# Four heads share one scaling in windowed attention, with earlier maxima in a fused feed-forward

## The chip, the cores and the metric

The kernel runs on one core of one Trainium2 chip. The metric is the device time of one execution in microseconds (us). Three runs of the kernel before gave 613.23, 614.52 and 616.42 us, so its median is 614.52 us.

## The reference

Two computations follow one another. The first is windowed attention: 4 batches, 8 heads, 768 positions, head size 64. Each query sees 8 global keys and the 96 latest keys up to itself, with a linear distance bias per head. The second is a feed-forward network on the 3072 x 512 result, with a leaky rectifier.

```python
scores = (1 / sqrt(64)) * q @ k.T + bias       # masked to 8 global and 96 local keys
a = exp(scores - max(scores)); a = a / (sum(a) + 1e-9)
x = (a @ v) as 3072 tokens x 512               # heads side by side
h = x @ w_in                                   # 512 -> 2048
g = maximum(h, 0) + alpha * minimum(h, 0)      # alpha per column
out = g @ w_out                                # 2048 -> 512
```

## The kernel before

The 3072 tokens are worked in twelve units u = 0 to 11 of 256 tokens. In a unit, each head h = 0 to 7 is attended (`attend`), the eight results stand side by side as `xn`, `xn` is transposed to `xt`, the first layer gives 16 blocks of 128 columns f = 0 to 15 and the second layer adds these 16 blocks up in two PSUM banks `o`. Almost every large product is three fp16 matmuls: a number is split into a high fp16 part (the "first copy", L342, L343, L351, L487) and the rest (L361, L362), and high by high, high by low and low by high are summed. The first two units keep fp32 in their attention and are transposed on TensorE; from unit 2 the transposes are DMAs.

**Attention.** TensorE makes scores `sp` (L609, L616), VectorE adds the bias and finds the extremum (L632), ScalarE exponentiates with a running sum (L637) into `pr`. In units 0 and 1, TensorE transposes `pr` into a bank `tp` (L657) and ScalarE copies that to `pt` (L661). `av` (L690) is the product with the values. The sums are inverted by two small VectorE instructions (L644, L646), and `xn` is `av` times the inverse (L699). `GROUP` says how many heads share one inversion and one multiplication.

**First layer.** For units 0 to 3, `ff_in2` makes two neighbouring blocks f in the two halves of one bank `h`, 12 matmuls each (L873). ScalarE (L342; L343 if it goes to VectorE) puts alpha times each half into `g`. VectorE takes the maximum with the whole bank (L881), and with it the bank is free. Then ScalarE casts the high part `gg` (L883) and VectorE makes the rest (L361). Units 0 and 1 have two banks with the tag `h`. From unit 4 on, `ff_in4` (L806 and on) uses sums of weight blocks `sw` and fewer products. The second layer is L897; L903 copies the finished bank and L906 stores it.

**Weights.** Each block f comes from memory as 64-bit numbers in two parts of 512 columns. Each part is turned into fp16 pairs by a first scaling `wf`, the bit work L478 (`wb`), L481 (`wb`) and L484 (`wf`) on VectorE, a first copy on ScalarE (L487) and the rest on VectorE (L362, `whl`). So a block costs VectorE eight instructions, beside units 0 and 1 only.

**Order.** Nothing is in loop order at the end. Every operation goes to a planner (`Plan`) with a key, a cost and the engine it may run on. The planner plays the program through with these costs: an engine that comes free takes the ready operation with the smallest key whose buffers are free, and the order found is the order that is written out. `slot` gives the key of a first-layer block; for unit 1 it stands `DELTA` behind unit 0's at the start and closer at the end. `mul` and `copy` belong to ScalarE, but the planner gives one to VectorE when ScalarE is far behind by its count (`FLEX`). So a changed key moves work between engines too. PSUM has eight banks: two `sp`, one `av`, one `ax`, two `h`, two `o`.

The squares (`energy`, L434) serve a check of the number range and are on ScalarE: `x_energy` squares a unit's `xt`, `weigh` the weights.

Of the kernel before, what the change touches and what calls it, by code (L numbers as in the profile page):

```python
# [23 lines left out]
P = 128  # L24
# [6 lines left out]
NU = 12  # L31
# [255 lines left out]
def c_dma(nbytes):  # L287
    return nbytes / 360.0
# [6 lines left out]
DELTA = 7  # L295
# [4 lines left out]
GROUP = (2, 2, 2, 2)  # L300
# [11 lines left out]
QLEAD = 2  # L312
SLEAD = 36
# [9 lines left out]
def fast(tc, cn, a):  # L323
    nc = tc.nc
    ctx = ExitStack()
    with ctx:
# [112 lines left out]
        def weigh(f, key):  # L439

            w = whl[f]
            for part in range(2):
                energy(key, lambda part=part: w.t[:, 0, 512 * part : 512 * part + 512], [(w, part)], NF * part + f, 512)
# [116 lines left out]
        def attend(u, h, key):  # L560
# [132 lines left out]
            works.append((cost, values, used))  # L693
            if n_ == G - 1:
                lag = 3 if plain else 4 if u == 2 else 5.5
                op("PE", key + lag, sum(x for x, _, _ in works) + 80, lambda: [x() for _, x, _ in works],
                   r=[x for _, _, y in works for x in y], w=[av])
# [7 lines left out]
        def x_transpose(u, qb, key):  # L705
# [18 lines left out]
            tp = buf(("av", "ax")[qb], f"xp{u}_{qb}", [P, 512])  # L724
# [12 lines left out]
        def x_energy(u, key):  # L737
            energy(key, lambda: xt[u].t[:, :NC, :].rearrange("p c t -> p (c t)"), [xt[u]], 2 * NF + u, 1024)
# [119 lines left out]
        def ff_in2(u, j, key, later):  # L858
# [22 lines left out]
            op("DVE", later, c_dve(2 * UT), lambda: v.scalar_tensor_tensor(  # L881
                out=g.t, in0=hp.t, scalar=KG, in1=g.t, op0=ALU.mult, op1=ALU.max), r=[hp], w=[g])
            op("ACT", later, c_act(2 * UT), lambda: nc.scalar.copy(out=gg.t[:, 0, :], in_=g.t), r=[g], w=[(gg, 0)])  # L883
            rest(later, lambda: gg.t[:, 1, :], lambda: g.t, None, lambda: gg.t[:, 0, :], [g, (gg, 0)], [(gg, 1)], 2 * UT)

        def ff_out(u, f, key):
# [4 lines left out]
            for t in range(2):  # L891
                o = acc[u][t]

                def products(t=t, o=o):
                    tok = slice(128 * t, 128 * t + 128)
                    for n, (g_, wi) in enumerate(((gh, 0), (gh, 1), (gl, 0))):
                        nc.tensor.matmul(o.t, lhsT=g_()[:, tok], rhs=w.t[:, wi, 512:1024],  # L897
                                         start=f == 0 and n == 0, stop=f == NF - 1 and n == 2)

                op("PE", key + 0.1 * t, 3 * 215.8, products, r=[*parts, (w, 1), (w, 3)], w=[o])  # L900
                if f == NF - 1:
                    s = buf("stage", f"os{u}_{t}", [P, 512])
                    op("ACT", key, c_act(512, True), lambda o=o, s=s: nc.scalar.mul(  # L903
                        out=s.t, in_=o.t, mul=OSC), r=[o], w=[s])
                    rows = u * UT + 128 * t
# [217 lines left out]
```

## Time and profile before

| | |
|---|---|
| median of the runs | 614.52 us |
| the profiled execution's own time | 615.02 us |
| its span | 613.1 us |
| mean granted TensorE clock | 0.994 of full speed |
| TensorE, busy | 589.9 us |
| VectorE, busy | 516.1 us |
| ScalarE, busy | 411.4 us |

The rows further down use the names PE for TensorE, DVE for VectorE, ACT for ScalarE, SP for the engine that issues most DMAs. The profiled execution's own time is 1.9 us longer than its span. In a row of a group of instructions stand the line, the engine, the operation and its tiles, the count, the busy time with the mean of one, and the idle time ahead with what ended it. The duration of one VectorE instruction overlaps the next one's start by some 0.08 us, so that where a queue is full the distance from start to start is what one costs.

### The profile page before, as it was taken

What the parts mean: (1) busy time and instruction counts of PE and PEld (TensorE: products, weight loads), DVE (VectorE), ACT (ScalarE), POOL (GpSimd) and SP (SyncE); (2) the same over time, 40 slices, a digit from 0 to 9 for tenths busy, and PEclk for the clock granted to TensorE, in tenths of its full rate; (3) what the DMA queues carried; (4) which work ended last, traced back from release to release, by engine and by line L of the source; (5) the groups of instructions that cost most, each with busy time, mean ns of one, the idle gap of its engine ahead of it and who ended that gap; (6) DMA issues with size and microseconds to landing.
All of it is one profiled execution on the core that took longest, in us unless ns stands there. A gap on an engine that the chain in (4) does not pass through costs nothing.

```text
span 613.1 us, 15956 instructions
## 1 busy us (share of the span) xinstructions
PE 589.9 (96%) x6212; PEld 415.4 (68%) x6212; DVE 516.1 (84%) x1437; ACT 411.4 (67%) x1082; POOL 1.6 (0%) x11
## 2 busy tenths in 40 slices
PE   8897999989999999999999999999999999999995
PEld 6775666556665666777777776777777777777762
DVE  7999899999999999899889788879889789655531
ACT  7787687766766677869669768768567767643421
POOL 1000000000000000000000000000000000000000
PEclk9899899999999999999999999999999999999999
DMA  8996325348536447756377567457488455313101
GB/s 304 412 367 231 95 59 131 79 82 176 117 103 149 102 117 122 175 116 121 91 154 148 97 146 123 91 147 140 81 145 153 116 104 112 74 33 61 36 1 40
DMA packets 133651, 78.98 MB, mean 129 GB/s; under 512 B 114880, under 2 KB 116416, under 8 KB 133568
## 3 DMA queue, kind: packets, MB, share of 16 engines
q1 hardware_dynamic: 133568, 77.89, 54.3%
q8 instruction: 50, 0.82, 0.6%
q14 instruction: 33, 0.27, 0.1%
HBM read 43.79 MB, written 6.29 MB: 82 GB/s over the span
## 4 chain that ended last, share of the span: by engine, by line
PE 64%; DVE 26%; DMA 4%; issue 3%; ACT 3%; SPq 0%; DVEq 0%; ACTq 0%
PE o L897 28%; PE hx L806 14%; PE hy L806 7%; PE av L690 4%; PE hz L806 3%; PE sp L609 3%; PE h L873 3%; DVE wb L481 2%; DVE wf L484 2%; DVE pr L632 2%; DVE whl L362 2%; DVE gg L361 2%; DVE g L881 2%; DVE ps L362 2%; DMA xt<-xs 1%
## 5 line engine op out<-in xcount | busy, mean ns | idle before, releaser
L897 PE MATMUL o<-whl,ghl 128*128 128x512 f16 x768 | 194.7, 379 | 1.0 <-DVE ghl L361 1.0
L806 PEld LDWEIGHTS <-sw 128*128 128x128 f16 x1536 | 93.5, 98 | 21.3 <-issue 0.2
L637 ACT ACTIVATE pr<-pr,sm 128x256 f32<-128x256 f32 (+1 forms) x192 | 92.5, 483 | 20.0 <-DVE sm L632 19.8
L897 PEld LDWEIGHTS <-ghl 128*128 128x128 f16 x768 | 66.4, 98 | 55.5 <-issue 4.9
L873 PE MATMUL h<-xt,whl 128*128 128x256 f16 x768 | 94.7, 277 | 8.8 <-DVE g L881 5.2
L873 PEld LDWEIGHTS <-whl 128*128 128x128 f16 x768 | 75.6, 100 | 28.1 <-issue 8.5
L897 PE MATMUL o<-whl,gg 128*128 128x512 f16 x384 | 92.8, 380 | 0.5 <-DVE gg L361 0.4
L806 PEld LDWEIGHTS <-whl 128*128 128x128 f16 x1152 | 71.2, 98 | 19.5 <-issue 0.2
L632 DVE CUSTOM_DVE_ANT_0 pr<-sp,D 128x256 f32<-128x256 f32 (+1 forms) x192 | 69.8, 396 | 12.3 <-PE sp L609 10.7
L814 ACT ACTIVATE g<-hx 128x256 f32<-128x256 f32 x96 | 36.5, 380 | 60.1 <-PE hx L806 59.7
L842 DVE SCALAR_TENSOR_TENSOR hs<-hs,alpha 128x256 f32<-128x256 f32 x128 | 58.4, 480 | 16.4 <-ACT hs L814 15.6
L897 PEld LDWEIGHTS <-gg 128*128 128x128 f16 x384 | 35.3, 98 | 40.6 <-DVE gg L361 4.6
L362 DVE SCALAR_TENSOR_TENSOR ps<-pr,ps 128x512 f16<-128x512 f32 (+1 forms) x80 | 51.3, 644 | 3.4 <-ACT ps L342 3.4
L361 DVE TENSOR_TENSOR ghl<-hs,ghl 128x512 f16<-128x512 f32 x64 | 41.9, 686 | 2.1 <-ACT ghl L849 2.1
L849 ACT CAST ghl<-hs 128x512 f16<-128x512 f32 x64 | 36.8, 613 | 2.3 <-DVE hs L842 2.3
L342 ACT ACTIVATE ps<-pr 128x512 f16<-128x512 f32 (+1 forms) x62 | 37.3, 602 | 1.2
L637 ACT ACTIVATION_READ_ACCUMULATOR pr<-pr,sm 128x1 f32 x192 | 36.5, 190 | 0.0
L342 ACT ACTIVATE g<-h,ak 128x256 f32<-128x256 f32 x59 | 27.2, 466 | 13.5 <-PE h L873 13.1
L690 PEld LDWEIGHTS <-vp 128*128 128x128 f16 x888 | 30.2, 98 | 3.7 <-issue 1.0
L690 PE MATMUL av<-vp 128*128 128x64 f16 x888 | 32.5, 193 | 0.0
L814 ACT ACTIVATE hs<-hx 128x256 f32<-128x256 f32 x32 | 12.1, 379 | 29.1 <-PE hx L806 29.0
L362 DVE SCALAR_TENSOR_TENSOR vp<-v,vp 128x256 f16<-128x256 f32 (+1 forms) x80 | 31.5, 396 | 0.0
(134 smaller groups left out, 865.9 us busy)
## 6 DMA issues: line engine op xcount, KB each, us to landing
w<-in_w_dram SPq DMA_DIRECT2D x32, 512.0 KB, 8.3
qk<-in_qk_dram SPq DMA_DIRECT2D x28, 336.0 KB, 3.3
v<-in_vw_dram SPq DMA_DIRECT2D x28, 256.0 KB, 3.5
out_dram<-os SPq DMA_DIRECT2D x24, 256.0 KB, 3.6
qk<-in_qk_dram SPq DMA_DIRECT2D x12, 272.0 KB, 2.9
v<-in_vw_dram SPq DMA_DIRECT2D x12, 192.0 KB, 3.1
first<-in_first_dram SPq DMA_DIRECT2D x4, 464.0 KB, 5.7
first<-in_first_dram SPq DMA_DIRECT2D x4, 336.0 KB, 9.8
```

The costliest lines, as they stand in the source:

```text
L342: lambda: nc.scalar.mul(out=out(), in_=src(), mul=by.t if tile_ else by)),
L361: return e.tensor_tensor(out=out(), in0=src(), in1=hi(), op=ALU.subtract)
L362: return e.scalar_tensor_tensor(out=out(), in0=src(), scalar=val(), in1=hi(), op0=ALU.mult, op1=ALU.subtract)
L632: op("DVE", key, c_dve(n) + 10, lambda qb=qb, n=n, dc=dc, pc=pc: v.tensor_tensor_reduce(out=pr.t[:, pc : pc + n], in0=sp.t[:, pc : pc + n] ...
L637: op("ACT", key + 1, c_act(n, ptr=1) + 93, lambda qb=qb, n=n, pc=pc: nc.scalar.activation(out=pr.t[:, pc : pc + n], in_=pr.t[:, pc : pc + ...
L690: nc.tensor.matmul(out, lhsT=p_[:, 128 * j : 128 * j + 128], rhs=v_[:, 64 * j : 64 * j + 64], start=m == 0, stop=m == len(ps) - 1)
L806: nc.tensor.matmul(bank.t[:, 128 * q : 128 * q + 128], lhsT=wt(q, wi, c), rhs=xp(xi, c), start=begin and q == n == 0, stop=n == 5, skip_gr ...
L814: op("ACT", k, c_act(UT, True), lambda: nc.scalar.mul(out=out(), in_=two(bank), mul=KG), r=[bank], w=w, spare=SPARE if u < NU - 1 else 0)
L842: op("DVE", ks[4 + 2 * i], c_dve(UT, ptr=True), lambda n=n: v.scalar_tensor_tensor(out=hs.t[:, n, :], in0=hs.t[:, n, :], scalar=alpha[:, 4 ...
L849: op("ACT", ks[6], c_act(512), lambda q=q, cols=cols: nc.scalar.copy(out=ghl.t[:, 0, cols], in_=flat(q)), r=src, w=[(ghl, q)])
L873: nc.tensor.matmul(hp.t[:, cols], lhsT=w.t[:, wi, wc], rhs=x.t[:, NC * xi + c, :], start=n == 0, stop=n == 3 * NC - 1)
L897: nc.tensor.matmul(o.t, lhsT=g_()[:, tok], rhs=w.t[:, wi, 512:1024], start=f == 0 and n == 0, stop=f == NF - 1 and n == 2)
```

## The change

- `GROUP` goes from 2 to 4 from unit 1 on: one inversion and one multiplication serve four heads. TensorE still makes `av` for two heads at a time; a bank `av` is held for four.
- `EV = 2`: the maximum (L881) and the cast (L883) of every pair in units 0 to 3 have a key that is smaller by 2, so the planner takes them ahead of weight conversions with a larger key.
- `DELTA` goes from 7 to 5.
- The transposed x of unit 0 (`xp`, L728) is in the two `h` banks instead of `av` and `ax`.
- The squares of x read nothing new but are held until the last weight block is converted; those of the weights until the sum `sw` of their pair exists.
- In the last unit's last block, the second layer's products are made in two halves of 256 columns per bank; ScalarE copies and stores the first half from its own queue, VectorE copies the second, which SP stores.

```diff
--- before.py
+++ after.py
@@ -292,12 +292,12 @@
 LEAD = 22
 LEAD0 = 30
 LEAD1 = 22
-DELTA = 7
+DELTA = 5
 WIDE = 1
 KP = 2
 DP = 3.5
 FLEX = {'ACT': 2, 'DVE': 1.5, 'POOL': 1}
-GROUP = (2, 2, 2, 2)
+GROUP = (2, 4, 4, 4)
 PT4 = 0
 DL = 3
 XDMA = 2
@@ -310,6 +310,7 @@
 US = 4
 QU = 4
 QLEAD = 2
+EV = 2
 SLEAD = 36
 SL = 3
 GLAG = 6.5
@@ -440,7 +441,7 @@
 
             w = whl[f]
             for part in range(2):
-                energy(key, lambda part=part: w.t[:, 0, 512 * part : 512 * part + 512], [(w, part)], NF * part + f, 512)
+                energy(key, lambda part=part: w.t[:, 0, 512 * part : 512 * part + 512], [(w, part), (sums[f // 2], 0)], NF * part + f, 512)
 
         def check(key):
             row = buf("av", "erow", [P, 512])
@@ -691,10 +692,12 @@
                                          start=m == 0, stop=m == len(ps) - 1)
 
             works.append((cost, values, used))
+            lag = 3 if plain else 4 if u == 2 else 5.5
+            if n_ % 2:
+                now, works[:] = list(works), []
+                op("PE", key + lag, sum(x for x, _, _ in now) + 80, lambda: [x() for _, x, _ in now],
+                   r=[x for _, _, y in now for x in y], w=[(av, n_)])
             if n_ == G - 1:
-                lag = 3 if plain else 4 if u == 2 else 5.5
-                op("PE", key + lag, sum(x for x, _, _ in works) + 80, lambda: [x() for _, x, _ in works],
-                   r=[x for _, _, y in works for x in y], w=[av])
                 cols = slice(64 * (h + 1 - G), 64 * (h + 1))
                 op("DVE", key + lag, c_dve(128 * G), lambda: v.tensor_tensor(
                     out=xn[u].t[:, :, cols].rearrange("p t (h d) -> p t h d", h=G),
@@ -721,7 +724,7 @@
 
                 op("SP", key, 115 * 8, transposes, r=[s], w=[(y, qb)])
                 return
-            tp = buf(("av", "ax")[qb], f"xp{u}_{qb}", [P, 512])
+            tp = buf(("av", "ax")[qb] if u else "h", f"xp{u}_{qb}", [P, 512])
 
             def transposes():
                 for c in range(NC):
@@ -735,7 +738,7 @@
                  [(y, 2 + qb)], 512)
 
         def x_energy(u, key):
-            energy(key, lambda: xt[u].t[:, :NC, :].rearrange("p c t -> p (c t)"), [xt[u]], 2 * NF + u, 1024)
+            energy(key, lambda: xt[u].t[:, :NC, :].rearrange("p c t -> p (c t)"), [xt[u], (whl[NF - 1], 3)], 2 * NF + u, 1024)
 
         def x_combine(u, key):
 
@@ -878,9 +881,10 @@
                 mul(k, lambda cols=cols: g.t[:, cols], lambda cols=cols: hp.t[:, cols], alpha_[f], [(hp, i), ak], [(g, i)],
                     "ACT", UT, True)
                 mo[u, f] = ((lambda cols=cols: gg.t[:, 0, cols]), (lambda cols=cols: gg.t[:, 1, cols]), [(gg, 0), (gg, 1)])
-            op("DVE", later, c_dve(2 * UT), lambda: v.scalar_tensor_tensor(
+            now = later - EV
+            op("DVE", now, c_dve(2 * UT), lambda: v.scalar_tensor_tensor(
                 out=g.t, in0=hp.t, scalar=KG, in1=g.t, op0=ALU.mult, op1=ALU.max), r=[hp], w=[g])
-            op("ACT", later, c_act(2 * UT), lambda: nc.scalar.copy(out=gg.t[:, 0, :], in_=g.t), r=[g], w=[(gg, 0)])
+            op("ACT", now, c_act(2 * UT), lambda: nc.scalar.copy(out=gg.t[:, 0, :], in_=g.t), r=[g], w=[(gg, 0)])
             rest(later, lambda: gg.t[:, 1, :], lambda: g.t, None, lambda: gg.t[:, 0, :], [g, (gg, 0)], [(gg, 1)], 2 * UT)
 
         def ff_out(u, f, key):
@@ -890,21 +894,39 @@
                 acc[u] = [buf(("sp", "ax")[t] if u == 1 else "o", f"o{u}_{t}", [P, 512]) for t in range(2)]
             for t in range(2):
                 o = acc[u][t]
-
-                def products(t=t, o=o):
-                    tok = slice(128 * t, 128 * t + 128)
-                    for n, (g_, wi) in enumerate(((gh, 0), (gh, 1), (gl, 0))):
-                        nc.tensor.matmul(o.t, lhsT=g_()[:, tok], rhs=w.t[:, wi, 512:1024],
-                                         start=f == 0 and n == 0, stop=f == NF - 1 and n == 2)
-
-                op("PE", key + 0.1 * t, 3 * 215.8, products, r=[*parts, (w, 1), (w, 3)], w=[o])
-                if f == NF - 1:
-                    s = buf("stage", f"os{u}_{t}", [P, 512])
-                    op("ACT", key, c_act(512, True), lambda o=o, s=s: nc.scalar.mul(
-                        out=s.t, in_=o.t, mul=OSC), r=[o], w=[s])
-                    rows = u * UT + 128 * t
-                    op("SP", key, c_dma(P * 2048), lambda s=s, rows=rows: nc.sync.dma_start(
-                        out=a["out"][rows : rows + 128, :], in_=s.t), r=[s])
+                parts_ = 2 if u == NU - 1 and f == NF - 1 else 1
+                n_ = 512 // parts_
+                s = buf("stage", f"os{u}_{t}", [P, 512]) if f == NF - 1 else None
+                rows = u * UT + 128 * t
+                for part in range(parts_):
+                    cols = slice(n_ * part, n_ * part + n_)
+
+                    def products(t=t, o=o, cols=cols):
+                        tok = slice(128 * t, 128 * t + 128)
+                        for n, (g_, wi) in enumerate(((gh, 0), (gh, 1), (gl, 0))):
+                            nc.tensor.matmul(o.t[:, cols], lhsT=g_()[:, tok],
+                                             rhs=w.t[:, wi, 512 + cols.start : 512 + cols.stop],
+                                             start=f == 0 and n == 0,
+                                             stop=f == NF - 1 and n == 2 and cols.stop == 512)
+
+                    op("PE", key + 0.1 * t + 0.05 * part, 3 * 0.4216 * n_, products, r=[*parts, (w, 1), (w, 3)],
+                       w=[(o, part) if parts_ > 1 else o])
+                    if f < NF - 1:
+                        continue
+                    r, z = [(o, part)], (s, part)
+                    if part == 0:
+                        op("ACT", key, c_act(n_, True), lambda o=o, s=s, cols=cols: nc.scalar.mul(
+                            out=s.t[:, cols], in_=o.t[:, cols], mul=OSC), r=r, w=[z])
+                    else:
+                        op("DVE", key, c_dve(n_), lambda o=o, s=s, cols=cols: v.tensor_scalar(
+                            out=s.t[:, cols], in0=o.t[:, cols], scalar1=OSC, scalar2=None, op0=ALU.mult), r=r, w=[z])
+                    on = nc.scalar if parts_ > 1 and part == 0 else nc.sync
+                    store = lambda on=on, s=s, rows=rows, cols=cols: on.dma_start(
+                        out=a["out"][rows : rows + 128, cols], in_=s.t[:, cols])
+                    if on is nc.sync:
+                        op("SP", key, c_dma(P * 4 * n_), store, r=[z])
+                    else:
+                        op("ACT", key, 100, store, r=[z])
 
         def warm(key):
 
```

The changed lines are numbered a little higher in the new program: L657 becomes L658, L690 becomes L691, L616 becomes L617, L728 becomes L731, L873 becomes L876, L881 becomes L885, L361/L362 become L362/L363, L478/L481/L484 become L479/L482/L485, L644/L646/L699 become L645/L647/L702, L903 becomes L918 and L921, L906 becomes L924.

A name in the following rows is a tile with its unit and index, as `h0_0` (first layer, unit 0, pair 0), and a running number behind it. On TensorE, between the scores of unit 1's third head and the first block of unit 0's first layer, there stood before:

```order
L616 MATMUL sp1_3_458<-first1_2_242 128x256 x2
L728 MATMUL xp0_0_465<-ident_58,xn0_335 128x128 x4
L728 MATMUL xp0_1_472<-ident_58,xn0_335 128x128 x4
L657 MATMUL tp1_1_496<-ident_58,pr1_1_405 128x128 x4
L873 LDWEIGHTS whl0_440
L873 MATMUL h0_0_505<-xt0_484,whl0_440 128x256
```

There stands now:

```order
L617 MATMUL sp1_3_457<-first1_2_242 128x256 x2
L731 MATMUL xp0_0_465<-ident_58,xn0_335 128x128 x4
L731 MATMUL xp0_1_472<-ident_58,xn0_335 128x128 x4
L658 MATMUL tp1_1_483<-ident_58,pr1_1_405 128x128 x4
L691 MATMUL av1_0_497<-firstv0_194,pt1_0_461 128x64 x4
L691 MATMUL av1_0_497<-firstv0_194,pt1_1_491 128x64 x4
L658 MATMUL tp1_2_513<-ident_58,pr1_2_477 128x128 x4
L617 MATMUL sp1_4_520<-first1_4_246 128x256 x2
L617 MATMUL sp1_5_523<-first1_4_246 128x256 x2
L876 LDWEIGHTS whl0_440
L876 MATMUL h0_0_533<-xt0_488,whl0_440 128x256
```

The transpose `tp1_1` no longer shares a bank with `xp0_1`, and the values and scores of unit 1 stand ahead of `h0_0`, which stood behind it.

On VectorE, around the maximum of pair 2 of unit 0 (`g0_2`), among the conversions of weight blocks 5 and 6, there stood before:

```order
L362 SCALAR_TENSOR_TENSOR whl5_877<-wf5_1_776,whl5_877 128x512
L484 SCALAR_TENSOR_TENSOR wf6_0_820<-w6_0_563,wb6_0_879 128x512
L481 SCALAR_TENSOR_TENSOR wb6_1_908<-w6_1_436,wb6_1_908 128x512
L881 SCALAR_TENSOR_TENSOR g1_0_860<-h1_0_825,g1_0_860 128x512
L362 SCALAR_TENSOR_TENSOR whl6_916<-wf6_0_820,whl6_916 128x512
L484 SCALAR_TENSOR_TENSOR wf6_1_868<-w6_1_436,wb6_1_908 128x512
L361 TENSOR_TENSOR gg1_0_922<-g1_0_860,gg1_0_922 128x512
L881 SCALAR_TENSOR_TENSOR g0_2_840<-h0_2_806,g0_2_840 128x512
```

There stands now:

```order
L362 TENSOR_TENSOR gg1_0_853<-g1_0_821,gg1_0_853 128x512
L363 SCALAR_TENSOR_TENSOR whl5_881<-wf5_0_743,whl5_881 128x512
L485 SCALAR_TENSOR_TENSOR wf5_1_782<-w5_1_363,wb5_1_874 128x512
L479 TENSOR_SCALAR wb6_0_907<-wf6_0_824 128x512
L479 TENSOR_SCALAR wb6_1_916<-wf6_1_859 128x512
L482 SCALAR_TENSOR_TENSOR wb6_0_907<-w6_0_601,wb6_0_907 128x512
L363 SCALAR_TENSOR_TENSOR whl5_881<-wf5_1_782,whl5_881 128x512
L485 SCALAR_TENSOR_TENSOR wf6_0_824<-w6_0_601,wb6_0_907 128x512
L482 SCALAR_TENSOR_TENSOR wb6_1_916<-w6_1_436,wb6_1_916 128x512
L885 SCALAR_TENSOR_TENSOR g1_1_889<-h1_1_861,g1_1_889 128x512
L363 SCALAR_TENSOR_TENSOR whl6_941<-wf6_0_824,whl6_941 128x512
L885 SCALAR_TENSOR_TENSOR g0_2_850<-h0_2_826,g0_2_850 128x512
```

The maximum and the rest of `g1_0` now stand a dozen rows further ahead, and at the place of `g0_2` unit 1 is one pair further on.

On VectorE, the inversions and multiplications of unit 3, with other work between them that is left out here, were before:

```order
L644 TENSOR_SCALAR sm3_0_1623<-sm3_0_1623 128x4
L646 RECIPROCAL sm3_0_1623<-sm3_0_1623 128x4
...
L699 TENSOR_TENSOR xn3_1981<-av3_0_1932,sm3_0_1623 128x2x128
...
L644 TENSOR_SCALAR sm3_2_1829<-sm3_2_1829 128x4
L646 RECIPROCAL sm3_2_1829<-sm3_2_1829 128x4
...
L699 TENSOR_TENSOR xn3_1981<-av3_2_2143,sm3_2_1829 128x2x128
```

and for the same four heads are now:

```order
L645 TENSOR_SCALAR sm3_0_1662<-sm3_0_1662 128x8
L647 RECIPROCAL sm3_0_1662<-sm3_0_1662 128x8
...
L702 TENSOR_TENSOR xn3_2153<-av3_0_1930,sm3_0_1662 128x2x256
```

Six instructions became three, with twice the elements in each.

## Rows read from the trace of the kernel before

**Rows 1.** The page's head: span, busy time by engine

```profile
span 613.1 us, 15956 instructions
PE 589.9 (96%) x6212; PEld 415.4 (68%) x6212; DVE 516.1 (84%) x1437; ACT 411.4 (67%) x1082; POOL 1.6 (0%) x11
```

**Rows 2.** Busy time by stretch: stretch, length, engines, granted clock, DMA share, GB/s

```profile
20.00:30.00 10.00, 7.17 (x49) 5.77 (x49) 9.64 (x27) 7.66 (x19) 0.00 (x0) 0.83 1.03 414
...
60.00:70.00 10.00, 8.24 (x48) 5.46 (x47) 7.79 (x15) 5.40 (x10) 0.00 (x0) 0.83 0.47 151
70.00:250.00 180.00, 174.55 (x1426) 114.21 (x1426) 176.25 (x458) 124.62 (x306) 0.00 (x0) 1.00 0.52 112
250.00:370.00 120.00, 120.00 (x1544) 87.53 (x1542) 104.38 (x308) 91.75 (x262) 0.00 (x0) 1.00 0.61 126
```

**Rows 3.** PE's waits: line, releaser, us in all, times, longest

```profile
PE h L873 <- DVE g L881: 5.2, 3, 2.7
PE tp L657 <- DVE xt L362: 2.8, 1, 2.8
PE h L873 <- ACT g L342: 2.0, 2, 1.1
```

**Rows 4.** Timeline of PE: start, us, instructions, [idle before <-releaser]

```profile
25.49 1.08 PE L657 MATMUL tp<-ident,pr 128*128 128x128 f32 x4 [2.83 <-DVE xt L362]
...
61.76 4.45 PE L873 MATMUL h<-xt,whl 128*128 128x256 f16 x24 [2.68 <-DVE g L881]
...
243.62 1.47 PE L873 MATMUL h<-xt,whl 128*128 128x256 f16 x12 [1.08 <-ACT g L342]
...
375.21 0.39 PE L897 MATMUL o<-whl,ghl 128*128 128x512 f16 x1 [0.97 <-DVE ghl L361]
```

**Rows 5.** Timeline of DVE, 59 to 247 us

```profile
59.22 0.68 DVE L362 SCALAR_TENSOR_TENSOR whl<-wf,whl 128x512 f16<-128x512 f32 x1
...
60.43 0.68 DVE L481 SCALAR_TENSOR_TENSOR wb<-w,wb 128x512 int32<-128x512 int32 x1
61.03 0.68 DVE L881 SCALAR_TENSOR_TENSOR g<-h,g 128x512 f32<-128x512 f32 x1
...
240.85 0.68 DVE L881 SCALAR_TENSOR_TENSOR g<-h,g 128x512 f32<-128x512 f32 x1
241.45 0.41 DVE L632 CUSTOM_DVE_ANT_0 pr<-sp,D 128x256 f32<-128x256 f32 x1
...
244.53 0.16 DVE L644 TENSOR_SCALAR sm<-sm 128x4 f32<-128x4 f32 x1
244.72 0.18 DVE L646 RECIPROCAL sm<-sm 128x4 f32<-128x4 f32 x1
244.82 0.68 DVE L362 SCALAR_TENSOR_TENSOR ps<-pr,ps 128x512 f16<-128x512 f32 x1
```

**Rows 6.** Groups of DVE: busy us, mean ns of one, idle before

```profile
L361 DVE TENSOR_TENSOR gg<-g,gg 128x512 f16<-128x512 f32 x32 | 21.8, 683 | 3.6 <-ACT gg L883 3.6
L699 DVE TENSOR_TENSOR xn<-av,sm 128x256 f32<-128x256 f32 x48 | 20.1, 419 | 2.7 <-PE av L690 2.1
L343 DVE TENSOR_SCALAR vp<-v 128x256 f16<-128x256 f32 x20 | 5.8, 289 | 3.7 <-PE av L690 3.7
L343 DVE TENSOR_SCALAR g<-h,ak 128x256 f32<-128x256 f32 x5 | 2.4, 478 | 0.3 <-PE h L873 0.3
```

**Rows 7.** Timeline of all engines, the program's end

```profile
603.76 3.18 PE L897 MATMUL o<-whl,ghl 128*128 128x512 f16 x14
...
606.34 1.24 ACT L903 ACTIVATE os<-o 128x512 f32<-128x512 f32 x2 [5.05 <-PE o L897]
```

**Rows 8.** The page: copy of half a bank; DMAs (count, KB each, us to landing)

```profile
L814 ACT ACTIVATE g<-hx 128x256 f32<-128x256 f32 x96 | 36.5, 380 | 60.1 <-PE hx L806 59.7
...
out_dram<-os SPq DMA_DIRECT2D x24, 256.0 KB, 3.6
...
v<-in_vw_dram SPq DMA_DIRECT2D x12, 192.0 KB, 3.1
```

## The prediction

> **What bounds the kernel now.** I read the page's head first. TensorE is busy in 589.9 of 613.1 us, VectorE in 516.1 [rows 1]. Read as an average, that says that TensorE bounds everything and that work taken from VectorE is worth nothing. So I went on to the busy time by stretch [rows 2]. From 70 to 250 us VectorE is busy in 176.25 of 180 us and from 20 to 30 us in 9.64 of 10, while TensorE has holes. From 250 to 370 us TensorE is busy in all of 120.00 us and VectorE has 15.6 us to spare. The kernel thus has two halves: up to about 250 us, with the weight conversions and the two-block first layer, VectorE sets the pace; behind that TensorE does. In the first half TensorE waits for few things: three times for the maximum that frees a first-layer bank (5.2 us), once behind x of unit 0 (2.8 us), twice for ScalarE's read of the other half of a bank (2.0 us) [rows 3]. The longest shows how it comes about. TensorE stopped at 59.1 us and went on at 61.76 [rows 4]. From 59.22 us on VectorE did three weight conversions, the last from 60.43, and began the maximum only at 61.03 [rows 5]. The last of these waits stands at 243.62, and after it comes one more of 0.97 us, at 375.21 [rows 4].
>
> So a microsecond of VectorE's work that goes away ahead of some 250 us is a microsecond of the end, as long as TensorE has its own work done by then. One behind it is worth nothing.
>
> **The change part by part.** I count what VectorE has in its queue ahead of the first row of unit 4's second-layer input (`ghl4_0`), where the first half ends, in the order of before and of the change, and price it from start to start, since a full queue overlaps the rows' durations: a 512-wide maximum costs 0.60 (240.85 to 241.45), an inversion pair 0.29 (244.53 to 244.82) [rows 5], a 256-wide multiplication by its mean less that overlap of 0.08, 0.335 [rows 6].
>
> Scaling for four heads: ahead of that point 23 inversion pairs become 13, 10 by 0.29 = 2.9 us. Of 22 multiplications of 256 columns 4 stay and 9 of 512 come: 18 by 0.335 = 6.0 go, 9 by 0.60 = 5.4 come (the 512-wide price is the maximum's, the nearest row). Together −3.5 us. The price is that x of a unit is complete 0.27 us later (0.60 for 0.335 in the last step), and that one bank holds four heads. Behind 250 us another 12 pairs go, worth nothing, TensorE being full.
>
> First copies: the planner gives VectorE 31 of them up to that point, 40 before. By kind, seven 256-wide copies of values by 0.20 (289 ns less the overlap [rows 6]) are 1.4; the others, by their widths at the same rate, 2.6 fewer and 1.6 more. Together −2.4 us, which ScalarE takes on: it is busy in 124.6 of 180 us [rows 2], so it has room.
>
> Work put behind: two score passes and two rests of units 5 and 6 now stand after that point, one step of unit 4 ahead of it. −1.6 us there; VectorE does it in its 15.6 spare us.
>
> The sum of VectorE's work is −7.5 us. Against it, TensorE's own order stands further back at the same point: 12 first-layer products of 128 columns and 12 score products that were ahead are now behind. Twelve products of 256 columns span 1.47 us [rows 4]; half the columns make 0.7 us for the first kind, and the scores, 128 or 256 columns each and two heads at a time, lie between 0.2 and 1.0. That costs back +0.9 to +1.7; I take +1.0, since before 243.62 TensorE's lag is partly the very waiting that goes.
>
> Earlier maxima (`EV`, `DELTA`): these take nothing from VectorE. They exchange places with conversions, and what is won is idle time. TensorE's 5.2 us in the first half are the symptom of VectorE's order, and are not added to the 7.5: as long as VectorE is full, TensorE only waits elsewhere. What counts is VectorE's own idle time in that half, 3.6 us ahead of the rest of `gg` [rows 6], in which the chain maximum, cast, rest had nothing behind it. It can go fully or not at all: 0 to −3.6, and I take −1.5, somewhat under the middle, because the new order also runs units 0 and 1 closer together in two banks.
>
> Unit 0's x in the `h` banks: the 2.83 us hole at 25.49 [rows 4] goes, and values and scores stand in it. It lies where VectorE is 96% busy [rows 2]; so TensorE does earlier what it had time for anyway. 0, with 0 to −0.4 (the rest of that stretch's 10 us). That both banks are taken costs nothing: the first block needs x itself, and the copies that free the banks are those that make x.
>
> Held squares: only unit 0's and 1's move on ScalarE, out of a stretch where it is not the bound. 0 either way.
>
> The wait at 375.21 goes or stays with a shift of phases: 0 to −0.97, taken at −0.5.
>
> The end: before, ScalarE copies the last two banks in 1.24 us [rows 7] and a store of 256 KB takes 3.6 us [rows 8]. Now the last bank is copied by ScalarE (380 ns for half [rows 8]) and then VectorE (478 [rows 6]), and the second waits for the first, as the two ends of a bank wait for each other in the first layer (1.08 us at 243.62 [rows 4]): 0.86 and a handover instead of 0.62. A store of half the size saves something: 192 KB land in 3.1 us against 256 in 3.6, though one is a load [rows 8]. So −0.5 for the store, +0.2 to +0.7 for the copies: −0.3 to +0.7 with the second queue's issue, taken at +0.2.
>
> The Trainium skill, "PSUM — Partial Sum Buffer", section "PSUM bank collisions raise a hardware error", says that two engines must be kept off one bank of PSUM at a time, even in disjoint columns. The wait of 1.08 us agrees. The rule speaks against the halves: splitting a bank buys no parallel copy, only a smaller store. By the skill's "DMA: Bandwidth & Descriptors", section "Anatomy of one DMA", a transfer is about 2.0 us of fixed cost and its bytes at 436 GB/s, fitted on another kind of queue; by it 256 KB would be 2.6 us, where the trace has 3.6, and the trace decides; only the difference is used, an estimate of 0.3 us for 128 KB less. With that the end would be +0.4 instead of +0.2.
>
> New waits: with VectorE relieved, something is late next. I expect the second unit's transposed x (its last VectorE step moves up by 2.1 us of queue, TensorE's by 2.6) and the weight blocks. From 0 to 2.8, the longest wait of its kind now [rows 3], taken at +0.8.
>
> Sum: −7.5 + 1.0 − 1.5 + 0 − 0.5 + 0.2 + 0.8 = −7.5. The profiled execution took 615.0 us, so 607.5; it lies 0.5 above the median of 614.5, to which the forecast is compared: **607.0 us**.
>
> **The rivals.** *Less gain.* Only removed instructions count: the shifted copies come back as waits for ScalarE, the idle time stays. Then −3.5 + 1.0 + 0.2, about 612, or with the postponed work half counted 611. For it speaks that the planner's own costs set the order and not these durations; against it ScalarE's free third.
>
> *More gain.* All 3.6 us of idle and the 0.97 go, and nothing new is late: −7.5 + 1.0 − 3.6 − 1.0 − 0.3 = −11.4, about 603.5. For it speaks that the maxima are ahead of conversions all along the stretch; against it that every earlier maximum delays a weight block.
>
> *Slower: units 0 and 1 in step.* They share two `h` banks for 16 pairs. With `DELTA` 5 and maxima taken first, VectorE may stand at a maximum whose bank TensorE has just begun to fill: it then idles for the half block and ScalarE's read, as TensorE does now for 1.08 us [rows 4], with weight conversions queued behind it. By my count the operand is ready only 0.5 to 1.3 us ahead in the new order. At 0.5 us for each of the 16 (8 us) the gain is gone; at 1.08 for each it is 17 − 7.5, about 624, and at 0.7 some 618. For it speaks how thin this slack is; against it that an engine that is late gives the slack back, and that VectorE, as the bound, is the late one.
>
> *It doesn't do what it says.* The squares hardly move and the halves at the end cost what they bring; both are in the sum at near nothing. If the maxima too change nothing, the first rival's time stands.
>
> **How the numbers follow.** The forecast has 0.50, less gain 0.22, more gain 0.18, in step 0.10. A median of this kernel tells about 0.5%, 3.1 us, from no change: faster is under 611.4, slower over 617.6. Faster takes the forecast (0.48 of it, as friction could eat it), more gain (0.18) and half of the less gain (0.11): 0.77. Slower is most of the last case: 0.07. Same is the rest, 0.16. The forecast's own bounds, with the unknown terms at their ends, are 604 and 611; with most of both neighbours the range is 602 to 613, which leaves out the slow case, the top of the less gain and the lowest tenth.
>
> **What would show it.** VectorE's busy time falls to about 508 us and 26 inversions stand where 48 did. TensorE's wait for the maximum falls from 5.2 us to under 2, and the 2.83 us behind x are gone. VectorE's idle time ahead of `gg` is about 2 us; TensorE becomes and stays full some 7 us sooner than after 243.62. The span ends 6.2 us after the last product, as now (613.1 against 603.76 + 3.18 [rows 7]). I am wrong if VectorE waits for `h` or `g` in units 0 and 1 by more than 5 us in all (in step), or if TensorE is full no sooner, or if holes come behind 250 us.

## The result, and the profile after

| | before | changed |
|---|---|---|
| median of six runs | 616.24 us | 608.89 us |
| ratio, 95% interval | | 0.9878, 0.9845 to 0.9912 |
| profiled execution: own time, span | 615.02, 613.1 us | 608.45, 606.7 us |

The changed kernel is faster by 1.2%, which on the 614.5 us of the forecast is 7.5 us, with 5.4 to 9.5 as the interval. The forecast was 7.5 us, to 607.0. The two profiled executions lie 6.6 us apart.

The head of the page of the changed kernel, in answer to [rows 1]:

```profile
span 606.7 us, 15901 instructions
PE 589.6 (97%) x6218; PEld 416.1 (69%) x6218; DVE 508.4 (84%) x1367; ACT 409.5 (68%) x1088; POOL 1.6 (0%) x11
```

TensorE's work is the same to 0.3 us; VectorE has 7.7 us less, close to the 508 us that were forecast. By stretch, in the columns of [rows 2]:

```profile
20.00:30.00 10.00, 8.83 (x74) 7.32 (x73) 9.96 (x31) 8.87 (x24) 0.00 (x0) 1.00 1.03 414
...
60.00:70.00 10.00, 10.00 (x69) 6.83 (x68) 10.00 (x23) 7.68 (x17) 0.00 (x0) 1.00 0.30 102
70.00:250.00 180.00, 174.81 (x1461) 115.03 (x1460) 171.83 (x429) 128.52 (x324) 0.00 (x0) 0.99 0.46 116
250.00:370.00 120.00, 120.00 (x1540) 87.10 (x1537) 104.10 (x295) 90.12 (x257) 0.00 (x0) 1.00 0.62 125
370.00:380.00 10.00, 10.00 (x118) 7.24 (x117) 9.93 (x30) 9.44 (x31) 0.00 (x0) 1.00 0.85 158
```

Between 20 and 70 us TensorE's holes shrank from 7.7 us to 2.5. From 70 to 250 it has as many as before, 5.2 us against 5.45. The hole at 375 us is gone. TensorE's waits changed owner, in answer to [rows 3]:

```profile
PE h L876 <- ACT g L343: 3.2, 4, 1.3
...
PE o L907 <- DVE gg L362: 1.3, 4, 0.5
...
PE sp L617 <- ACT os L918: 1.2, 1, 1.2
```

No wait for a maximum is left among those of a microsecond and more, and none for unit 0's x as a whole bank. Three groups of VectorE answer to [rows 6]:

```profile
L362 DVE TENSOR_TENSOR gg<-g,gg 128x512 f16<-128x512 f32 x32 | 21.9, 685 | 1.1 <-ACT gg L887 1.1
...
L702 DVE TENSOR_TENSOR xn<-av,sm 128x512 f32<-128x512 f32 x22 | 15.1, 688 | 1.8 <-PE av L691 1.2
L647 DVE RECIPROCAL sm<-sm 128x8 f32<-128x8 f32 x22 | 4.5, 203 | 0.8
```

One multiplication with twice the columns costs 688 ns instead of two at 419. The cleanest view of the change is a stretch that ends at a fixed place in the program: from 20 us to the start of the first rest of unit 4's second-layer input, which is the place to which the prediction counted. Before:

```profile
20.00:261.84 241.84, 228.71 (x1928) 156.36 (x1928) 232.71 (x597) 171.96 (x421) 0.00 (x0) 0.99 0.58 152
```

and with the change:

```profile
20.00:254.20 234.20, 226.50 (x1890) 154.76 (x1889) 225.25 (x555) 170.95 (x421) 0.00 (x0) 0.99 0.53 156
```

The place is reached 7.64 us sooner. VectorE's busy time in it (the third pair of numbers) is 7.46 us less, its idle time 8.95 us instead of 9.13. From this place to TensorE's last product it takes 345.1 us before and 345.4 after.

The end of the program with the change, all engines, in answer to [rows 7]:

```profile
595.73 3.85 PE L907 MATMUL o<-whl,ghl 128*128 128x512 f16 x23
...
598.96 0.38 ACT L918 ACTIVATE os<-o 128x256 f32<-128x256 f32 x1 [5.06 <-PE o L907]
...
599.38 0.42 DVE L921 TENSOR_SCALAR os<-o 128x256 f32<-128x256 f32 x1 [4.67 <-ACT os L918]
...
599.86 0.38 ACT L918 ACTIVATE os<-o 128x256 f32<-128x256 f32 x1 [0.52 <-PE o L907]
...
600.27 0.42 DVE L921 TENSOR_SCALAR os<-o 128x256 f32<-128x256 f32 x1 [0.47 <-ACT os L918]
```

The last product ends at 599.58, and the span 7.1 us later; before it was 6.2. The two copies of a bank stand one behind the other, VectorE's beginning 0.03 us after ScalarE's end.

### The profile page after: what moved, and what is told of

Same layout as the page of the kernel before. It is cut to its first block, busy times and chain, and to the rows that moved or that the text cites. A ratio compares the mean times of both kernels' runs of the same rounds, so it can differ in the third digit from the quotient of the medians.

```text
span 606.7 us, 15901 instructions
## 1 busy us (share of the span) xinstructions
PE 589.6 (97%) x6218; PEld 416.1 (69%) x6218; DVE 508.4 (84%) x1367; ACT 409.5 (68%) x1088; POOL 1.6 (0%) x11
## 4 chain that ended last, share of the span: by engine, by line
PE 75%; DVE 19%; ACT 3%; issue 2%; DMA 1%; ACTq 0%; DVEq 0%
PE o L907 33%; PE hx L809 14%; PE hy L809 7%; PE h L876 7%; PE av L691 4%; PE hz L809 4%; PE sp L610 3%; PE sp L617 2%; DVE g L885 2%; DVE pr L633 2%; DVE gg L362 2%; DVE wf L485 1%; DVE whl L363 1%; DVE wb L482 1%; ACT pr L638 1%
## 5 line engine op out<-in xcount | busy, mean ns | idle before, releaser
L907 PE MATMUL o<-whl,ghl 128*128 128x512 f16 (+1 forms) x774 | 193.8, 378 | 0.0
L876 PE MATMUL h<-xt,whl 128*128 128x256 f16 x768 | 93.2, 276 | 4.5 <-ACT g L343 3.2
L876 PEld LDWEIGHTS <-whl 128*128 128x128 f16 x768 | 75.0, 99 | 23.8 <-issue 7.3
L363 DVE SCALAR_TENSOR_TENSOR ps<-pr,ps 128x512 f16<-128x512 f32 (+1 forms) x80 | 51.2, 644 | 5.9 <-ACT ps L343 5.7
L362 DVE TENSOR_TENSOR ghl<-hs,ghl 128x512 f16<-128x512 f32 x64 | 42.1, 686 | 2.2 <-ACT ghl L852 2.1
L343 ACT ACTIVATE ps<-pr 128x512 f16<-128x512 f32 (+1 forms) x58 | 34.8, 600 | 0.9
L691 PEld LDWEIGHTS <-vp 128*128 128x128 f16 x888 | 30.4, 98 | 3.1 <-issue 0.4
L691 PE MATMUL av<-vp 128*128 128x64 f16 x888 | 32.4, 193 | 0.0
L363 DVE SCALAR_TENSOR_TENSOR vp<-v,vp 128x256 f16<-128x256 f32 (+1 forms) x80 | 31.3, 397 | 0.0
```

Of the source, the lines that this page charges most:

```text
L343: lambda: nc.scalar.mul(out=out(), in_=src(), mul=by.t if tile_ else by)),
L362: return e.tensor_tensor(out=out(), in0=src(), in1=hi(), op=ALU.subtract)
L363: return e.scalar_tensor_tensor(out=out(), in0=src(), scalar=val(), in1=hi(), op0=ALU.mult, op1=ALU.subtract)
L691: nc.tensor.matmul(out, lhsT=p_[:, 128 * j : 128 * j + 128], rhs=v_[:, 64 * j : 64 * j + 64], start=m == 0, stop=m == len(ps) - 1)
L876: nc.tensor.matmul(hp.t[:, cols], lhsT=w.t[:, wi, wc], rhs=x.t[:, NC * xi + c, :], start=n == 0, stop=n == 3 * NC - 1)
L907: nc.tensor.matmul(o.t[:, cols], lhsT=g_()[:, tok], rhs=w.t[:, wi, 512 + cols.start : 512 + cols.stop], start=f == 0 and n == 0, stop=f == ...
```

## The experiments

Two theories stood against each other. By "work", the end follows the work that VectorE has queued ahead of the place named above. By "order", it follows TensorE's waits for the maxima, and VectorE's work as such has spare room. The table holds, for each kernel, what the order counts as VectorE's work ahead of the place, when the place was reached, VectorE's busy and idle time from 20 us to it, the time from TensorE's last product to the end of the span, and the ratio of the times to those of the kernel before.

| kernel | counted | reached at | busy | idle | end | ratio, 95% interval |
|---|---|---|---|---|---|---|
| before | 248.4 | 261.84 | 232.7 | 9.1 | 6.2 | 1 |
| changed | 240.9 | 254.20 | 225.3 | 9.0 | 7.1 | 0.9878, 0.9845 to 0.9912 |
| e1_group2 | 245.9 | 257.01 | 231.6 | 5.4 | 6.8 | 0.9937, 0.9914 to 0.9960 |
| e2_ev0 | 242.2 | 255.62 | 227.3 | 8.4 | 6.7 | 0.9921, 0.9892 to 0.9951 |
| e3_xp_av_ax | 242.2 | 255.99 | 226.9 | 9.1 | 6.7 | 0.9924, 0.9897 to 0.9952 |
| e4_whole_store | 240.9 | 253.49 | 226.2 | 7.3 | 6.1 | 0.9884, 0.9850 to 0.9918 |
| e5_early_work | 251.6 | 268.06 | 236.2 | 11.9 | 7.0 | 1.0068, 1.0037 to 1.0098 |
| e6_late_work | 240.9 | 252.34 | 224.9 | 7.4 | 7.2 | 0.9880, 0.9839 to 0.9922 |
| e7_only_group4 | 242.8 | 256.38 | 227.0 | 9.4 | 6.1 | 0.9901, 0.9865 to 0.9937 |
| e8_only_ev2 | 245.5 | 257.27 | 229.3 | 8.0 | 5.9 | 0.9950, 0.9921 to 0.9978 |
| e9_squares | 242.3 | 254.32 | 226.7 | 7.6 | 6.8 | 0.9936, 0.9910 to 0.9962 |
| e10_delta7 | 242.1 | 255.22 | 227.0 | 8.2 | 7.2 | 0.9919, 0.9889 to 0.9949 |
| e11_flex3_whole | 238.5 | 253.39 | 224.9 | 8.5 | 5.9 | 0.9890, 0.9854 to 0.9926 |
| e12_flex4_whole | 236.6 | 255.63 | 223.1 | 12.5 | 5.9 | 0.9922, 0.9894 to 0.9949 |

For e5 the count holds the added work at its measured 10.7 us. In all fourteen traces TensorE needs 345.1 to 345.9 us from the place to its last product. What differs between two kernels is therefore the time at which the place is reached, and the end.

Two things limit what the table can tell. Each time in it is that of one execution. The changed kernel, e4 and e6 have the same order of instructions on TensorE, VectorE and ScalarE up to the place, and reached it at 254.20, 253.49 and 252.34, so differences of up to 1.9 us say little. And the times carry TensorE's granted clock. In the 66 runs of the kernel before that stood beside the experiments, the mean clock of a run lies between 0.986 and 0.997 of full speed and its time between 612.4 and 620.0 us, the longer times at the lower clocks. Straight lines with one slope for all kernels, through the 177 runs whose clock is on record, give 4.9 us for 0.01 of the clock. Read off these lines at one clock, the estimates are 5.7 us for the change, 4.1 for e7 and 2.5 for e8, each with 0.5 to 0.7 of uncertainty, and 9.2 ± 0.9 for what e5 costs against the changed kernel. Their order stays, and up to 2.5 us of the differences below go with the clock. Whether the new orders bring a higher clock or met it by chance, the runs do not separate.

**Work added, early and late (e5, e6).** Both add the same 36 instructions on a buffer that nothing reads, behind the inversions of units 1 to 3 or of units 6 to 8; the order of everything else is the same. The first group runs at 27.7 us in the early kernel and at 280.3 in the late one, the last at 172.4 and at 390.6.

```diff
+        scr = one.tile([P, 128], F32, name="scr")
...
                 v.reciprocal(out=sm.t[:, 6 * G :], in_=sm.t[:, 4 * G : 6 * G])
+                if u in (1, 2, 3):                     # e6: (6, 7, 8)
+                    for _ in range(6):
+                        v.scalar_tensor_tensor(out=scr, in0=scr, scalar=KG, in1=scr, op0=ALU.mult, op1=ALU.max)
+                if u == 0 and h == 1:
+                    v.memset(scr, 0.0)
```

> The changed kernel with 36 more VectorE instructions of 128 columns (on a buffer that nothing reads), six behind each inversion of units 1 to 3, so all ahead of 250 us; the order of everything else is unchanged. At 0.2 us each VectorE gets 7.2 us more work. Theory 'work': the end comes 5 to 7 us later (a part goes into idle time), 614 to 616 where the changed kernel has 608.9. Rival 'order' (TensorE and the banks set the pace in the first half too): under 2 us later.

> The same 36 instructions behind the inversions of units 6 to 8, so behind 250 us. Theory 'work': nothing, 608 to 610, because TensorE is full there and VectorE has room. Rival (VectorE bounds everywhere): 7 us later.

Measured: early 619.52 us, a ratio 0.0190 above that of the changed kernel, 11.7 us; late 607.26 us, no difference. One group of six on VectorE's timeline in the early kernel, with the rows before and after it, tells what they cost:

```profile
106.72 0.20 DVE L648 RECIPROCAL sm<-sm 128x8 f32<-128x8 f32 x1
106.84 1.87 DVE L651 SCALAR_TENSOR_TENSOR scr<-scr 128x128 f32<-128x128 f32 x6
108.63 0.75 DVE L480 TENSOR_SCALAR wb<-wf 128x512 int32<-128x512 int32 x2
```

From 106.84 to 108.63 are 0.30 us for each, not the 0.2 that I had assumed, so 36 are 10.7 us. The early kernel pays 11.7, with an uncertainty of 2.8 that follows from the two intervals. Its runs had a mean granted clock of 0.991 against 0.9945 in the changed kernel; at one clock it pays 9.2, so most of the added work is paid, and perhaps all. The stretch to the place in the early kernel:

```profile
20.00:268.06 248.06, 234.59 (x1897) 160.54 (x1897) 236.19 (x592) 172.21 (x425) 0.00 (x0) 0.97 0.51 148
```

has 10.9 us more VectorE work than in the changed kernel. That its profiled execution is 13.7 us longer is partly a lower granted clock, 0.97 over the stretch. The late kernel has the same added group in its own row of groups:

```profile
L651 DVE SCALAR_TENSOR_TENSOR scr<-scr 128x128 f32<-128x128 f32 x36 | 10.2, 284 | 1.0
```

and loses nothing. This settles "work" against "order": VectorE's work has a price in the first half and none in the second. Where between 174 and 280 us the border lies, these two do not tell.

**One part alone on the kernel before (e7, e8).** The edits are shortened.

```diff
-GROUP = (2, 2, 2, 2)
+GROUP = (2, 4, 4, 4)          # e7, with the values still made for two heads at a time
...
-            op("DVE", later, ... g.t ...)      # maximum; the cast likewise
+            op("DVE", later - 2, ... g.t ...)  # e8
```

> The kernel before with the scaling for four heads alone. Theory 'work': VectorE's queue ahead of unit 4's second-layer input falls by 5.6 us (248.4 to 242.8), TensorE stands 1.1 us further back: 4 to 5 us faster than before, ratio about 0.993. Rival 'order': nothing, since TensorE's waits for the maxima stay: ratio 1.000.

> The kernel before with the earlier keys for maxima and casts alone. Theory 'work': the queue falls by 2.9 us (248.4 to 245.5), TensorE stands 1.1 us further back, VectorE's idle time of 3.6 us goes in part: 2 to 4 us faster, ratio 0.994 to 0.997. Rival 'order': the waits of 5.2 us go and the time with them, ratio 0.991.

Scaling for four heads alone gives 0.9901, 6.1 us, and the earlier maxima alone 0.9950, 3.1 us. TensorE's waits and its timeline in e7 show that its gain did not come by ending the waits:

```profile
PE h L875 <- DVE g L883: 5.7, 5, 1.9
...
24.98 0.63 PE L657 MATMUL tp<-ident,pr 128*128 128x128 f32 x4 [2.90 <-DVE xt L362]
...
52.21 2.79 PE L875 MATMUL h<-xt,whl 128*128 128x256 f16 x24 [1.78 <-DVE g L883]
...
60.76 2.79 PE L875 MATMUL h<-xt,whl 128*128 128x256 f16 x24 [1.86 <-DVE g L883]
```

The hole behind x is there, 2.90 us, and so are the waits for maxima, 5.7 us in all against 5.2 before [rows 3], and the kernel is faster nevertheless, by 6 us, or by 4 at one clock. VectorE has 5.7 us less to do ahead of the place. For e8 the count said 2.9 and the trace 3.4 us.

**One part taken out of the change (e1, e2, e3, e9, e10).**

```diff
-GROUP = (2, 4, 4, 4)
+GROUP = (2, 2, 2, 2)                              # e1
-EV = 2
+EV = 0                                            # e2
-            tp = buf(("av", "ax")[qb] if u else "h", ...)
+            tp = buf(("av", "ax")[qb], ...)       # e3
-                energy(key, ..., [(w, part), (sums[f // 2], 0)], NF * part + f, 512)
+                energy(key, ..., [(w, part)], NF * part + f, 512)      # e9
-            energy(key, ..., [xt[u], (whl[NF - 1], 3)], 2 * NF + u, 1024)
+            energy(key, ..., [xt[u]], 2 * NF + u, 1024)                # e9
-DELTA = 5
+DELTA = 7                                         # e10
```

> The changed kernel with GROUP back at 2 for every unit; the rest of the change stays. Theory 'work' (the time follows the work that VectorE has queued ahead of unit 4's second-layer input): by the order this work rises by 5.0 us (240.9 to 245.9, 3.5 of it inversions and multiplications), so about 4 to 5 us slower than the changed kernel, 612 to 614 where the changed kernel has 608.9. Rival 'order' (the gain is the earlier maxima, which ended TensorE's 5.2 us of waits): no change within 1 us, about 609.

> The changed kernel with EV = 0, so that maxima and casts have the key of before. Theory 'work': VectorE's queue ahead of unit 4's second-layer input rises by 1.3 us (240.9 to 242.2), and some of its idle time ahead of the rests comes back: 1 to 3 us slower, 610 to 612. Rival 'order': TensorE waits for the maxima again, 5 us slower or more, 614.

> The changed kernel with unit 0's transposed x in the banks av and ax again. Theory 'work': TensorE's hole of 2.8 us at 25 us comes back, VectorE's queue rises by 1.3 us (planner's moves), so 1 to 2 us slower. Rival 'hole': the whole 2.8 us come back or more, 612. A third possibility: nothing.

> The changed kernel with the squares not held back. The prediction put the edit at nothing. By the order, though, the planner then gives VectorE more: its queue ahead of unit 4's second-layer input rises by 1.4 us (240.9 to 242.3). Theory 'work': 1 to 1.5 us slower than the changed kernel, ratio to before about 0.990. Rival (squares are hidden on ScalarE): 0.988, nothing.

> The changed kernel with DELTA at 7 again. The queue ahead of unit 4's second-layer input rises by 1.2 us (240.9 to 242.1). Theory 'work': 1 to 1.5 us slower, ratio 0.990. Rival 'in step' (units 0 and 1 closer together cost waits): faster than the changed kernel by up to 1 us, 0.986.

Against the changed kernel the five cost 3.6, 2.6, 2.8, 3.6 and 2.5 us by their ratios, each with 2.5 to 2.8 us of uncertainty. e1 and e9 are clear of zero, e3 barely, e2 and e10 are not. That they add up to twice the gain says that they are not shares of it. The traces, read against the changed kernel's own execution, carry more: the place is reached 2.8 us later without the scaling for four, with 6.3 us more VectorE work, of which 3.5 went into what had been idle time. Of that idle time, 1.6 us stood behind a stretch at a low clock in the changed kernel's execution (last section):

```profile
20.00:257.01 237.01, 227.04 (x1907) 155.25 (x1907) 231.57 (x595) 171.08 (x423) 0.00 (x0) 1.00 0.57 155
```

Without the earlier maxima it is 1.4 us later, with the old banks 1.8, with the old `DELTA` 1.0, each with 1.7 to 2.0 us more VectorE work. Against the places of e4 and e6 these three come 2.1 to 3.3, 2.5 to 3.7 and 1.7 to 2.9 us later. In e3 the 2.9 us hole in TensorE is back, and with it 1.7 us of VectorE's work; the two prices are not told apart. For the squares the trace, 0.1 us later, and the times, 3.6 us slower, do not agree; its profiled execution was the fastest of its nine. Against e4 and e6 its place comes 0.8 and 2.0 us later, about what the count of 1.4 says. So holding the squares back seems to be worth something, by the work that the planner moves; how much stays open.

**The end (e4).**

```diff
-                parts_ = 2 if u == NU - 1 and f == NF - 1 else 1
+                parts_ = 1
```

> The changed kernel with the last two banks copied and stored whole, as before. From the two traces: the span ended 7.1 us after the last product with halves and 6.2 us without, so I expect 0.5 to 1.0 us faster than the changed kernel (about 608.1), nothing else moved. Rival (smaller stores land sooner): 0.3 us slower.

The times, 608.18 us and 0.9884, cannot tell 0.7 us. The traces can: in the eight profiles with halves, 6.7 to 7.2 us pass from the last product to the end of the span, in the six with whole banks 5.9 to 6.2. The halves cost 0.9 us on the mean. Half of that are the copies: the last one ends 1.1 us after the last product, before it was 0.6. The stores give nothing back. The changed kernel's four, with the last one by itself in the third row, against 3.6 us for 256 KB [rows 8]:

```profile
out_dram<-os ACTq DMA_DIRECT2D x2, 128.0 KB, 1.7
out_dram<-os SPq DMA_DIRECT2D x1, 128.0 KB, 1.7
...
out_dram<-os SPq DMA_DIRECT2D x1, 128.0 KB, 3.7
```

Three halves landed 1.7 us after their issue. The last, on which the end hangs, took 3.7, as long as a whole bank; in six of the eight profiles with halves it took 3.1 to 3.9. In the other two, e1 and e2, it took 1.7 to 1.8, and the span then ended 3.8 to 3.9 us after it landed instead of 2.0 to 2.4. From the end of the last copy to the end of the span it thus takes 5.5 to 6.1 us with halves and 5.3 to 5.5 with whole banks. What holds the end back, no view shows; the second queue that is then in use is a guess.

**Going further the same way (e11, e12).** Both store whole banks, and the planner gives first copies to VectorE more reluctantly.

```diff
-FLEX = {'ACT': 2, 'DVE': 1.5, 'POOL': 1}
+FLEX = {'ACT': 2, 'DVE': 3, 'POOL': 1}            # e12: 4
```

> A version of my own: the changed kernel with the last banks stored whole, and the planner gives a first copy to VectorE only when ScalarE is twice as far behind as now (FLEX of DVE 3 instead of 1.5). VectorE's queue ahead of unit 4's second-layer input falls by 2.4 us (240.9 to 238.5). Theory 'work': 2 us faster for that and up to 1 us for the store, ratio 0.983 to 0.985. Rival: ScalarE, busy for 128 of 180 us from 70 to 250, is late with its copies and VectorE waits for it: no gain or a loss, 0.988 to 0.995.

> The same with FLEX of DVE 4: the queue falls by 4.3 us (240.9 to 236.6). Theory 'work': 4 to 5 us faster than the changed kernel, ratio 0.980. Rival: the waits for ScalarE grow and the gain ends before this point, ratio that of the version with 3 or worse.

Neither beats the changed kernel: 607.62 us, 0.9890, and 610.21, 0.9922. Of the 2.4 us of VectorE's work that e11 takes away by the count, its trace shows 0.3. In e12 VectorE has 2.1 us less to do in the stretch and is idle 3.6 us more:

```profile
20.00:255.63 235.63, 227.43 (x1900) 155.96 (x1900) 223.12 (x546) 174.85 (x435) 0.00 (x0) 0.99 0.53 156
```

Its timeline has VectorE waiting for the copies that ScalarE took on:

```profile
32.88 0.69 DVE L363 SCALAR_TENSOR_TENSOR whl<-wf,whl 128x512 f16<-128x512 f32 x1 [0.98 <-ACT whl L488]
...
106.00 0.69 DVE L363 SCALAR_TENSOR_TENSOR whl<-wf,whl 128x512 f16<-128x512 f32 x1 [1.10 <-ACT whl L488]
...
227.85 0.69 DVE L885 SCALAR_TENSOR_TENSOR g<-h,g 128x512 f32<-128x512 f32 x1 [1.63 <-ACT g L343]
```

So work added to the changed kernel has its price, and work taken away no longer pays: VectorE waits for ScalarE instead. No version that I ran is clearly faster than the changed kernel; the best of them, e11 and e4, differ from it by less than the intervals.

## Why the prediction was right

It named the mechanism and the place: VectorE's work has a price in the first half and none behind it (e5, e6), the gain comes without TensorE's waits ending (e7), and from the place to the last product all traces take 345.1 to 345.9 us. The size was right too, but that a sum of 7.5 met a measured 7.5 is partly luck: the profiled executions lie 6.6 us apart, and the estimate at one clock is 5.7. By its terms:

- **VectorE's work, −7.5.** The trace has −7.46 in the stretch to the place. Scaling for four alone took 5.7 of VectorE's time there in e7, more than its own 3.5. The planner moved the rest with it, two bias passes and two rests to behind the place, and gave VectorE one first copy less. The split into parts was thus not the sum's strong side; the total was.
- **TensorE further back, +1.0.** From the place to the last product it takes 345.38 us against 345.10, and 0.97 of the latter was the hole at 375.21: +1.25.
- **VectorE's idle time, −1.5.** This term failed in the profiled execution: 0.2 instead of 1.5. The 3.6 us ahead of the rests fell to 1.1, but new idle came, 2.43 us at 149 us in one piece, behind a stretch at a low granted clock (below). In e4 and e6, which have the same order to there and no such stretch, the idle time is 1.7 to 1.9 us below that of before. The forecast read all of the 3.6 us as the chain of maximum, cast and rest. But 2.21 of them stand in one piece at 67.26, behind 24 products that took 4.45 us [rows 4] at a granted clock of 0.57 (62 to 66 us), where 24 take 2.79 in e7.
- **The hole at 375 us, −0.5.** It went whole, −0.97.
- **The end, +0.2.** It cost 0.9, above the bound of 0.7 that I had given. The second copy waited for the first as forecast, which is half of the 0.9. The −0.5 for a shorter store did not come: the last half took 3.7 us to land where a whole bank had taken 3.6.
- **New waits, +0.8.** I had expected them at the second unit's x. TensorE waits there 0.82 us at 46.82, where before it had waited 1.47 us for weight blocks at 50.28 and 51.07. The new ones, 1.55 us, stand at scores behind unit 1's output and at unit 2's x. What they cost is part of VectorE's idle time and can't be added to it.
- **The two terms at 0.** e3 and e9 say that x's banks and the held squares were not worth nothing, 2.8 and 3.6 us with 2.7 and 2.6 of uncertainty, each measured by taking it out of the change. The count has 1.3 and 1.4 us of VectorE's work for them, which the forecast has among its first copies.

The timeline of all engines with the change shows the new waits:

```profile
141.73 0.60 ACT L918 ACTIVATE os<-o 128x512 f32<-128x512 f32 x1 [2.08 <-DMA out_dram<-os]
...
142.38 0.92 PE L617 MATMUL sp<-qk 64*128 64x128 f32 x4 [1.22 <-ACT os L918]
...
143.63 7.08 PE L876 MATMUL h<-xt,whl 128*128 128x256 f16 x48 [0.33 <-DMA xt<-xs]
```

Only 0.33 us of them are x. The larger one, 1.22 us, is the copy of unit 1's output, which holds a score bank and itself waits 2.08 us for a store to free its buffer. I had not seen that one.

The errors are +1.3 for the idle time, +0.7 for the end, +0.25 for TensorE, −0.5 for the hole, −0.8 for the new waits, which came within the idle time. They cancel in part, to +1.0, which is what the spans say: 6.4 us where 7.5 were forecast. That the forecast met the median to within 2 us is therefore better than its terms were.

Of the rivals, "less gain" would have been 2.5 to 3.5 us and "more gain" 11; the measured interval of 5.4 to 9.5 reaches neither. "In step" did not come: VectorE waits for a half's copy in units 0 and 1 once, for 0.26 us. TensorE is full from 225 us on, its last wait of the first half being

```profile
225.01 1.47 PE L876 MATMUL h<-xt,whl 128*128 128x256 f16 x12 [0.64 <-ACT g L343]
```

in place of 243.62 [rows 4]. That is 18 us sooner where I had said 7; the wait at 243.62 was of its own kind, and its going is not the gain.

## What to carry to other kernels

Where two engines take turns as the bound, price a change by the work that it removes ahead of the place at which the turn passes, and find that place first: here added work of VectorE's was paid ahead of it, 10.7 us with 9.2 to 11.7, and cost nothing behind it, while a gain came with the other engine's waits in place. The exchange is not exact, since idle time takes up some of the difference (6.3 us more in e1 put the place 2.8 us back), and a wait can still cost time by the clock behind it, as the next section shows. A planner that moves work between engines makes the count in the written order worth more than the diff, since an edit of a key moved up to 2.9 us of VectorE's work. And when a bound has been relieved by some per cent, expect the next step in the same direction to find another engine there.

## What the runs showed of the hardware that I had not expected

Small VectorE instructions that each read what the one before wrote cost 0.30 us at 128 columns of fp32 in e5 (six in 1.79 us), while in e6 a bias pass of the same width is followed after 0.21 to 0.22 by the next, which does not read it. The bias passes are another operation, so that the reading is the reason is not shown.

The same order of instructions met a lower clock in one execution and not in another. Granted clock (the third number from the end; 1 is 2.4 GHz, and the other level, 0.5, is 1.2 GHz) of the changed kernel while 48 first-layer products of unit 2 run, taking 7.08 us:

```profile
143.00:151.00 8.00, 7.67 (x66) 6.02 (x65) 5.47 (x18) 5.18 (x16) 0.00 (x0) 0.79 0.74 191
```

and of e6, whose order is the same to there:

```profile
143.00:149.00 6.00, 5.69 (x62) 5.07 (x62) 5.06 (x16) 4.61 (x15) 0.00 (x0) 1.00 0.95 250
```

where they take 5.41 us:

```profile
142.15 0.92 PE L618 MATMUL sp<-qk 64*128 64x128 f32 x4 [1.25 <-ACT os L924]
143.38 5.41 PE L882 MATMUL h<-xt,whl 128*128 128x256 f16 x48 [0.31 <-DMA xt<-xs]
```

TensorE had waited 1.55 and 1.56 us just before, as good as the same. What decides whether the 1.7 us are lost, the traces do not show. They are paid, although VectorE sets the pace in this half: in the changed kernel ScalarE waits 2.81 us for these products (at 148.07), and VectorE for the exponentials that ScalarE has behind that. VectorE's wait in the changed kernel and in e6:

```profile
149.06 0.36 DVE L344 TENSOR_SCALAR ps<-pr 128x384 f16<-128x384 f32 x1 [2.43 <-ACT pr L638]
...
147.21 0.36 DVE L344 TENSOR_SCALAR ps<-pr 128x384 f16<-128x384 f32 x1 [0.83 <-ACT pr L639]
```

From the bias pass that starts at 132.45 us in the one and at 132.19 in the other it is 121.75 us to the place and 120.15. So the low clock cost 1.6 us here. In the kernel before, the waits of 2.83 and 2.68 us [rows 4] each came with such a stretch: the granted clock is 0.83 from 20 to 30 and from 60 to 70 us [rows 2].
